# Summing two blocks by an accumulating transfer instead of on VectorE, in an FNet and SwiGLU kernel on one core

## The chip, the core and the metric

The kernel runs on one core of a Trainium2 chip. The metric is the device time of one execution in microseconds; three runs of the kernel before took 674.59 to 674.76, median 674.68. The engines are TensorE (PE; PEld is its loading of weights), VectorE (DVE), ScalarE (ACT), GpSimd (POOL) and SyncE (SP), which here only issues transfers. Transfers are issued by SP, POOL and ACT, each into a queue of its own, and carried out by 16 DMA engines that all queues share.

## The reference

```python
g = sigmoid((x * gate_w).sum(-1))                      # x: 2048 x 512, float32
a, b = x @ dft_hid_re.T, x @ dft_hid_im.T
y = dft_seq_re @ a - dft_seq_im @ b                    # two 2048 x 2048 transforms
h = silu(x @ w1) * (x @ w3)                            # 512 x 1376 each
return g * y + (1 - g) * (h @ w2)
```

Everything is float32. The two transforms commute; the kernel applies the one along the sequence first, with real and imaginary matrix, and the one along the hidden dimension to its results.

## The kernel before, in words

A float32 product is made of three float32r products: each operand is split into a high part (ScalarE, `high`, line 110) and a low part (VectorE, `low`, line 113), and `mm3` adds high by high, high by low and low by high. On top of that each product of 2 x 2 blocks is made with seven block products instead of eight, in Winograd's way, so that sums of blocks such as T1 = B12 + B11 are needed as operands.

The work has three phases: gate and up products of the feed-forward part (up to about 207 us), the sequence transform (block numbers 0 to 3 of the kernel's list of eight, kind "F"), and then the down product ("H", blocks 4 and 5) and the transform along the hidden dimension ("Y", 6 and 7). The change touches the "F" blocks 1 to 3.

An "F" block has 28 steps: seven products in the order P1, P5, P6, P3, P7, P2, P4 (block 0 has P2 ahead of P7), each over four pieces q = 0 to 3 of the contraction. A step has 12 matmuls of 128x512 and one moving operand "z", 128x1024 in high and low part (`ZT`, tiles `zo`, four buffers). The operands come from the four raw blocks B11, B12, B21, B22 of the transform's matrix (input `cc`), 512 KB per piece, in the tiles `RAW` (shown as B in the profile). Product P5, steps 4 to 7 of a block, uses T1 = B12 + B11, summed in B12's own tile; P6 uses T2 = T1 + B22 in the same tile; P7 uses T3 = T2 - B11, so B11 itself is kept; P4 uses T4.

The order of the work is written out by hand. Step m of all steps first runs the list of things that are due (`todo`), then issues its matmuls, and then `advance(m)`, which prepares later steps: `load_c(m + 8)` issues the loads that are due for step m + 8, on SP's queue, as far as tiles are free; `sum_c(m + 4)` makes the sum for step m + 4 on VectorE; `split_c(m + 3)` splits the operand of step m + 3. Since there are four z buffers, the high part for step m + 3 waits until the matmuls of step m - 1 are through.

The loads' list `LOADS` gives each raw piece a step by which it is due: the four of B12 of a block become due in the three steps before its P5 and the first of it, and are asked for up to eight steps earlier.

GpSimd's queue carries in these blocks the results: `spill` (line 818) stores the four results of a block into `zsp`, in the order zu, zp, zs, zc (in block 0 zs comes ahead of zp); zc is the last thing of a block's last step, after `advance`; `gates` (lines 769 and 770) stores the gates, once in block 0 and once in block 1; and in blocks 1 and 2 `late_store` (line 800) stores pre-split weights for the later phases, from the `todo` list and so ahead of the step's `advance`. Each of these transfers waits on GpSimd for the engine that made its data, and all that stands behind it in the program waits with it.

Of the kernel before, what the change touches and what calls it, by code (L numbers as in the profile page):

```python
# [10 lines left out]
ALU = mybir.AluOpType  # L11
# [4 lines left out]
F = 1376  # L16
# [17 lines left out]
def fnet_swiglu_gate_kernel(  # L34
# [21 lines left out]
    nc = tc.nc  # L56
# [41 lines left out]
    def wide(name):  # L98
        return take(F4, [P, 1024], F32, name)
# [4 lines left out]
    def free(*tiles):  # L104
        for t in tiles:
            _, places, at = HELD.pop(id(t))
            places.append(at)
# [490 lines left out]
    for k in range(LOOK + 2):  # L598
# [18 lines left out]
    KIND = "F" * NTB + "HHYY"  # L617
# [3 lines left out]
    STEPS = [(blk, q, k, form) for blk, nq in enumerate(NQ) for k, form in ORDER[blk]  # L621
             for q in range(nq)]
# [8 lines left out]
    LEAD = 3  # L631
# [4 lines left out]
    RAW, ZT = {}, {}  # L636
# [3 lines left out]
    def z_rows(tb, k):  # L640
        return zsp[(tb * 4 + k) * P : (tb * 4 + k + 1) * P, :]

    def block(blk, k, q):
        if KIND[blk] == "F":
            return cc[blk, ("B11", "B12", "B22", "B21").index(k), q]
        if KIND[blk] == "H":
            return hsp[blk - NTB, ("B11", "B12", "B21", "B22").index(k), q]
        return z_rows(2 * (blk - NTB - 2) + (k in ("B12", "B22")), 2 * (k in ("B21", "B22")) + q)

    def cols(blk, q, form):  # L650

        return 512 if KIND[blk] == "H" and q == NQ[blk] - 1 else 1024

    def done(m, j):
        blk, q, k, form = STEPS[m]
        b = DONE[j].get(form)
        if b:
            free(RAW.pop((blk, b, q)))

    def sum_c(m):  # L660


        if not 0 <= m < len(STEPS):
            return
        blk, q, k, form = STEPS[m]
        b = {"T1": "B11", "T2": "B22", "T4": "B21"}.get(form)
        if b:
            n = cols(blk, q, b)
            t = RAW[blk, PLACE[form], q][:, :n]
            nc.vector.tensor_add(t, t, RAW[blk, b, q][:, :n])  # L670
        elif form == "T3":
            n = cols(blk, q, form)
            t = RAW[blk, "B11", q][:, :n]
            nc.vector.tensor_sub(t, RAW[blk, "B12", q][:, :n], t)  # L674
        done(m, 0)

    def split_c(m, parts_of=(0, 1)):
        if not 0 <= m < len(STEPS):
            return
        blk, q, k, form = STEPS[m]  # L680
        src = RAW[blk, PLACE.get(form, form), q]
        if 0 in parts_of:
            ZT[m] = parts(f"zo{m}")
        t = ZT[m].rearrange("p h a n -> p h (a n)")
        n = cols(blk, q, form)
        if 0 in parts_of:
            high(t[:, 0, :n], src[:, :n])
        if 1 in parts_of:
            low(t[:, 0, :n], t[:, 1, :n], src[:, :n])
            done(m, 1)  # L690

    def load_c(m):
        while LOADS and LOADS[0][0] <= m and F4:
            _, blk, k, q = LOADS.pop(0)
            r = RAW[blk, k, q] = wide(f"{k}_{blk}_{q}")
            n = cols(blk, q, k)
            nc.sync.dma_start(r[:, :n], block(blk, k, q)[:, :n])

    def advance(m):
        load_c(m + LEAD + AHEAD)  # L700
        sum_c(m + LEAD + 1)
        split_c(m + LEAD)

# [47 lines left out]
    high_a(NG - 1)  # L751
    low_a(NG - 1)
    advance(-1)
    load_score(0)

# [118 lines left out]
    def step(m):  # L874
# [30 lines left out]
        for r in range(2):  # L905
            sl = slice(r * P, (r + 1) * P)
            for dst, some, new in banks_of(r) if steps else ():
                for n, zn in steps:
                    for i in range(ni):
# [4 lines left out]
                            some)  # L914
        free(zt)
        advance(m)
        if q < NQ[blk] - 1:
            return
# [155 lines left out]
    for i, (src, sp, p) in enumerate(late):  # L1074
        blk, b = 1 + i // 3, i % 3
# [106 lines left out]
```

## Time and profile before

| | us |
|---|---|
| median of three runs | 674.68 |
| profiled execution | 674.39 |
| its span, first to last instruction | 672.6 |
| PE busy in the span | 667.5 |
| DVE busy | 577.5 |
| ACT busy | 369.9 |
| POOL busy | 61.8 |

Busy times come from the profile's page, which describes one execution. A row of the groups or of the timeline names the engine, the line of the kernel, the operation and `out<-in` by the program's tile names; many operations are recorded at the line of a helper (110, 113, 124, 697), so tiles tell them apart. "POOLq" and "SPq" are issues of transfers, and the last number in such a row is the time in us from issue to landing. "<-" behind a row's idle time names what ended it. In the tables by stretch, each engine's busy time is followed by the number of its instructions, and the last three columns are the granted share of TensorE's clock, the mean busy share of the 16 DMA engines and the bytes that they moved in GB/s.

### The profile page before, as it was taken

What the parts mean: (1) busy time and instruction counts of PE and PEld (TensorE: products, weight loads), DVE (VectorE), ACT (ScalarE), POOL (GpSimd) and SP (SyncE); (2) the same over time, 40 slices, a digit from 0 to 9 for tenths busy, and PEclk for the clock granted to TensorE, in tenths of its full rate; (3) what the DMA queues carried; (4) which work ended last, traced back from release to release, by engine and by line L of the source; (5) the groups of instructions that cost most, each with busy time, mean ns of one, the idle gap of its engine ahead of it and who ended that gap; (6) DMA issues with size and microseconds to landing.
All of it is one profiled execution on the core that took longest, in us unless ns stands there. A gap on an engine that the chain in (4) does not pass through costs nothing.

```text
span 672.6 us, 8611 instructions
## 1 busy us (share of the span) xinstructions
PE 667.5 (99%) x3101; PEld 580.5 (86%) x3101; DVE 577.5 (86%) x684; ACT 369.9 (55%) x471; POOL 61.8 (9%) x114
## 2 busy tenths in 40 slices
PE   9999999999999999999999999999999999999997
PEld 6888888888888888888888888888888888888886
DVE  6979877787679999988999799869798698798896
ACT  6765556656546874465454655444446446445452
POOL 0011112121110000101120101000000010010000
PEclk9999999999999999999999999999999999999999
DMA  7675655599986957744697267619889795784942
GB/s 296 217 300 223 236 216 208 203 352 376 424 358 249 363 186 239 249 154 158 234 379 293 83 255 274 280 34 355 303 332 228 255 357 170 312 299 175 340 126 94
DMA packets 46010, 171.23 MB, mean 255 GB/s; under 512 B 5520, under 2 KB 5904, under 8 KB 42256
## 3 DMA queue, kind: packets, MB, share of 16 engines
q1 hardware_dynamic: 33376, 118.90, 49.8%
q0 software_dynamic: 12160, 51.13, 19.4%
q10 hardware_dynamic: 432, 0.66, 0.3%
q8 instruction: 24, 0.39, 0.2%
q14 instruction: 18, 0.15, 0.1%
HBM read 115.34 MB, written 55.32 MB: 254 GB/s over the span
## 4 chain that ended last, share of the span: by engine, by line
PE 99%; DMA 1%; ACT 0%; SPq 0%; issue 0%
PE P L124 68%; PE X L124 16%; PE Z L124 8%; PE Y L124 4%; PE C L124 2%; DMA xs_B<-xt 1%; PE V L124 0%; PE P4left L124 0%; ACT xo L110 0%; ACT zc L835 0%; SPq L223 0%
## 5 line engine op out<-in xcount | busy, mean ns | idle before, releaser
L124 PE MATMUL P<-zo,a 128*128 128x512 f32 x1344 | 290.3, 379 | 0.0
L110 ACT ACTIVATE zo<-B 128x1024 fp32r<-128x1024 f32 (+1 forms) x182 | 185.5, 1022 | 182.8 <-PE P L124 99.9
L124 PEld LDWEIGHTS P<-zo,a 128*128 128x128 f32 x1344 | 253.9, 189 | 36.2
L113 DVE TENSOR_TENSOR zo<-B,zo 128x1024 fp32r<-128x1024 f32 (+1 forms) x182 | 213.8, 1180 | 33.1 <-ACT zo L110 32.4
L670 DVE TENSOR_TENSOR B<-B,B 128x1024 f32<-128x1024 f32 (+1 forms) x78 | 91.8, 1177 | 0.1
L124 PE MATMUL P<-zo,H 128*128 128x512 f32 x420 | 91.3, 379 | 0.0
L124 PEld LDWEIGHTS P<-zo,H 128*128 128x128 f32 x420 | 79.2, 189 | 11.8 <-issue 0.7
L124 PE MATMUL X<-xo,wb 128*128 128x512 f32 x378 | 88.7, 379 | 0.0
L124 PEld LDWEIGHTS X<-xo,wb 128*128 128x128 f32 x378 | 71.3, 189 | 10.4 <-DMA wb<-wbsp 0.2
L124 PE MATMUL P<-zo,Y 128*128 128x512 f32 (+1 forms) x336 | 71.6, 375 | 0.0
L124 PEld LDWEIGHTS P<-zo,Y 128*128 128x128 f32 x336 | 62.7, 189 | 8.7
L385 ACT ACTIVATE h<-X 128x512 f32<-128x512 f32 x21 | 12.5, 596 | 36.0 <-PE X L124 36.0
L323 POOL DMA_DIRECT2D hsp<-h x40 | 21.9, 547 | 112.0 <-DVE h L374 66.6
L124 PE MATMUL Z<-xo,wb 128*128 128x512 f32 x126 | 30.9, 380 | 0.0
L674 DVE TENSOR_TENSOR B<-B,B 128x1024 f32<-128x1024 f32 (+1 forms) x26 | 30.6, 1178 | 0.0
L124 PE MATMUL Z<-xo,wa 128*128 128x512 f32 x126 | 30.6, 379 | 0.0
L124 PE MATMUL X<-xo,wa 128*128 128x512 f32 x126 | 30.5, 379 | 0.0
L124 PE MATMUL Y<-xo,wa 128*128 128x512 f32 x126 | 30.5, 379 | 0.0
L124 PEld LDWEIGHTS Z<-xo,wb 128*128 128x128 f32 x126 | 23.7, 189 | 3.7 <-DVE xo L113 0.4
L124 PEld LDWEIGHTS Y<-xo,wa 128*128 128x128 f32 x126 | 23.8, 189 | 3.4
L124 PEld LDWEIGHTS Z<-xo,wa 128*128 128x128 f32 x126 | 23.8, 189 | 3.4
L124 PEld LDWEIGHTS X<-xo,wa 128*128 128x128 f32 x126 | 23.8, 189 | 3.4
(158 smaller groups left out, 549.0 us busy)
## 6 DMA issues: line engine op xcount, KB each, us to landing
B<-cc SPq DMA_DIRECT2D x64, 512.0 KB, 6.3
hsp<-h POOLq DMA_DIRECT2D x40, 256.0 KB, 4.0
wbsp<-wb POOLq DMA_DIRECT2D x8, 1024.0 KB, 4.2
wb<-wbsp SPq DMA_DIRECT2D x8, 1024.0 KB, 8.1
B<-hsp SPq DMA_DIRECT2D x16, 512.0 KB, 8.5
B<-zsp SPq DMA_DIRECT2D x16, 512.0 KB, 7.4
ws<-w SPq DMA_DIRECT2D x11, 512.0 KB, 5.6
H<-w2sp SPq DMA_DIRECT2D x5, 1024.0 KB, 8.5
```

Source lines behind the costliest of these rows:

```text
L110: nc.scalar.activation(hi, src, AF.Copy)
L113: nc.vector.tensor_sub(lo, src, hi.bitcast(F32))
L124: nc.tensor.matmul(ps.rearrange("p (n a) -> p n a", a=2), u, turns(v)[:, some], **kw)
L323: nc.gpsimd.dma_start(hsp[g, b + k, j // 2, :, j % 2 * 512 : (j % 2 + 1) * 512], h)
L385: nc.scalar.activation(g1, x, AF.Silu)
L670: nc.vector.tensor_add(t, t, RAW[blk, b, q][:, :n])
L674: nc.vector.tensor_sub(t, RAW[blk, "B12", q][:, :n], t)
```

## The change

For the blocks 1 to 3 of kind "F", and the form T1 alone, `sum_c` does nothing. Instead a new function `add_c`, called in `advance` two steps ahead of where the sum stood and between the loads and the sums, issues a transfer on GpSimd's queue that reads B11 from HBM a second time and adds it into the tile of B12. That is 12 transfers of 512 KB in place of 12 instructions of VectorE. GpSimd has to wait for B12's load before it issues one, and ScalarE and VectorE wait for its landing before they split the sum. The T1 sums of block 0 and of the blocks of the other kinds stay on VectorE.

```diff
+    def by_dma(blk, form):
+        return KIND[blk] == "F" and blk > 0 and form == "T1"
+
+    def add_c(m):
+
+        if not 0 <= m < len(STEPS):
+            return
+        blk, q, k, form = STEPS[m]
+        if by_dma(blk, form):
+            nc.gpsimd.dma_start(RAW[blk, "B12", q], block(blk, "B11", q), accum_op=ALU.add)
+
     def sum_c(m):
...
         b = {"T1": "B11", "T2": "B22", "T4": "B21"}.get(form)
-        if b:
+        if by_dma(blk, form):
+            pass
+        elif b:
             n = cols(blk, q, b)
...
     def advance(m):
         load_c(m + LEAD + AHEAD)
+        add_c(m + LEAD + 3)
         sum_c(m + LEAD + 1)
         split_c(m + LEAD)
```

## The prediction

> **What bounds the kernel now.** I read the page first, then the chain of waits, then the busy time by stretches. On the page the chain that ended last lies on TensorE nearly everywhere:
>
> ```profile
> span 672.6 us, 8611 instructions
> PE 667.5 (99%) x3101; PEld 580.5 (86%) x3101; DVE 577.5 (86%) x684; ACT 369.9 (55%) x471; POOL 61.8 (9%) x114
> ...
> PE 99%; DMA 1%; ACT 0%; SPq 0%; issue 0%
> ```
>
> In order of time (start, length, what), that chain holds one unbroken run of matmuls from the start of the sequence transform on, and the matmuls of its four blocks fill their stretch:
>
> ```profile
> 206.95 325.92 PE P L124 x1510
> ```
>
> ```profile
> 206.95:497.03 290.08, 290.08 (x1345) 253.93 (x1345) 14.77 (x23) 18.49 (x32) 1.00 0.66 244
> ```
>
> The four blocks have 4 x 28 = 112 steps of 12 matmuls, so a step takes 290.08 / 112 = 2.590 us, and step m starts at 206.95 + 2.590 m. By block (columns: stretch, length, then PE, PEld, DVE, ACT and POOL busy, granted clock, DMA share, GB/s):
>
> ```profile
> 207.00:279.50 72.50, 72.50 (x337) 63.41 (x336) 70.95 (x75) 46.14 (x53) 3.74 (x7) 1.00 0.74 261
> 279.50:352.00 72.50, 72.50 (x337) 63.48 (x337) 66.90 (x76) 41.54 (x49) 9.46 (x18) 1.00 0.64 238
> 352.00:424.70 72.70, 72.70 (x338) 63.66 (x338) 66.89 (x72) 37.43 (x44) 6.71 (x13) 1.00 0.63 240
> 424.70:497.00 72.30, 72.30 (x337) 63.31 (x336) 59.40 (x57) 33.33 (x36) 2.14 (x4) 1.00 0.64 236
> ```
>
> TensorE has no gap in any block, so nothing that VectorE gives back there can shorten the run. The question is only whether the new transfers land before TensorE asks for their sums.
>
> **What is removed.** In blocks 1 to 3, 4 sums each: 12 of the 72 instructions of this row.
>
> ```profile
> L670 DVE TENSOR_TENSOR B<-B,B 128x1024 f32<-128x1024 f32 x72 | 87.7, 1218 | 0.1
> L113 DVE TENSOR_TENSOR zo<-B,zo 128x1024 fp32r<-128x1024 f32 x168 | 204.3, 1221 | 31.3 <-ACT zo L110 30.6
> ```
>
> 12 x 1.218 = 14.6 us of VectorE, 4.9 us a block. Beside a TensorE that never waits this is worth 0; it cannot be less than 0, nor more while PE reads 72.50 of 72.50.
>
> **What is added: 12 issues on GpSimd.** A plain issue there takes 0.53 to 0.55 us (start, length, what; idle time before it in brackets):
>
> ```profile
> 277.67 0.53 POOL L818 DMA_DIRECT2D zsp<-zp  x1 [3.07 <-DVE zp L816]
> 281.14 0.53 POOL L818 DMA_DIRECT2D zsp<-zc  x1 [2.94 <-DVE zc L816]
> ```
>
> ```profile
> 349.35 0.53 POOL L800 DMA_DIRECT2D dsp<-late_0l  x1 [0.93 <-DVE u2p L177]
> 350.63 0.55 POOL L800 DMA_DIRECT2D dsp<-late_1h  x1 [0.74 <-ACT late_1h L110]
> 351.69 0.55 POOL L800 DMA_DIRECT2D dsp<-late_1l  x1 [0.51 <-DVE late_1l L113]
> 355.17 0.54 POOL L818 DMA_DIRECT2D zsp<-zc  x1 [2.93 <-DVE zc L816]
> ```
>
> ```profile
> 418.27 0.54 POOL L818 DMA_DIRECT2D zsp<-zs  x1 [8.59 <-DVE zs L816]
> 425.88 0.55 POOL L818 DMA_DIRECT2D zsp<-zc  x1 [7.08 <-DVE zc L816]
> ```
>
> If an adding issue costs one to two plain ones, 12 take 6 to 13 us of an engine that is busy 9%; worth 0. The order matters more. `add_c` runs in the last two steps of the block before and the first two of its own, so the queue reads: zp, add 0, add 1, zc, add 2, add 3 (block 1); late_0l, add 0, late_1h, late_1l, add 1, zc, add 2, add 3 (block 2, where the late stores stand ahead of `step` in the same turns); zs, add 0, add 1, zc, add 2, add 3 (block 3). The first adds go out at about 278.2, 349.9 and 419.
>
> The added wait is for the block B12 that is to be added to. The four B12 loads of blocks 1, 2 and 3 are issued from 259 to 264, 338 to 345 and 410.5 to 416.5, and land in (median):
>
> ```profile
> B<-cc SPq DMA_DIRECT2D x4, 512.0 KB, 5.3
> ```
>
> ```profile
> B<-cc SPq DMA_DIRECT2D x4, 512.0 KB, 8.6
> ```
>
> ```profile
> B<-cc SPq DMA_DIRECT2D x4, 512.0 KB, 8.0
> ```
>
> In blocks 1 and 2 they are there when GpSimd reaches the add. In block 3 it waits until about 419.5 and 421; behind it stands only zc, which isn't asked for before 425.88. Worth 0.
>
> **When the sums are needed.** ScalarE makes the high part of a block 3 steps ahead, and VectorE the low part behind it (1.22 us, row L113 above):
>
> ```profile
> 282.16 1.06 ACT L110 ACTIVATE zo<-B 128x1024 fp32r<-128x1024 f32 x1 [1.58 <-PE P L124]
> ```
>
> That is step 32, the first with T1 of block 1 (its matmuls start at 206.95 + 82.88 = 289.83). The sum may come late by up to the cushion, and must land by the step's start less 1.06 + 1.22 = 2.3 us: 287.5, 290.1, 292.7, 295.3 in block 1 (steps 32 to 35), 360.0, 362.6, 365.2, 367.8 in block 2 (60 to 63), 432.6, 435.2, 437.8, 440.3 in block 3 (88 to 91). From issue to need there are only 9 to 13 us. A sum that is late holds up ScalarE and VectorE, whose next work (the copies of P1, the T2 sums) has 4 steps or more in hand, and TensorE, by what is missing.
>
> **When they land.** From the end of one block into the next the DMA engines are full, and then idle (columns as above):
>
> ```profile
> 289.00:294.00 5.00, 5.00 (x25) 4.36 (x25) 3.81 (x4) 4.29 (x7) 0.00 (x0) 1.00 0.00 0
> ...
> 349.00:358.00 9.00, 9.00 (x43) 7.87 (x43) 9.00 (x10) 4.83 (x5) 2.17 (x4) 1.00 1.02 404
> ...
> 419.00:425.20 6.20, 6.20 (x30) 5.44 (x29) 4.50 (x5) 2.76 (x3) 0.00 (x0) 1.00 1.03 413
> ...
> 432.00:440.00 8.00, 8.00 (x39) 7.01 (x38) 7.29 (x8) 4.24 (x5) 0.00 (x0) 1.00 0.01 3
> ```
>
> Full, they move about 0.41 MB a us, so 512 KB (0.524 MB) take 1.28 us. Call the work of one adding transfer c times that of a plain one of its size. No row shows one. It can't be below c = 1 (0.524 MB come in from HBM as in a load of B) and two whole transfers, c = 2, are my upper end. I take 1.5: a plain packet is read and written, this one is read twice and written, three passes for two.
>
> [...]
>
> What lies before each queue, in MB, in three stretches (282 to 289, 358 to 368, 425.2 to 435; q1 is SyncE's, q0 GpSimd's):
>
> ```profile
> q1 hardware_dynamic: 505, 1.55, 54.8%
> q0 software_dynamic: 288, 1.05, 36.6%
> ```
>
> ```profile
> q1 hardware_dynamic: 858, 2.86, 77.8%
> q0 software_dynamic: 33, 0.09, 2.7%
> ```
>
> ```profile
> q1 hardware_dynamic: 679, 2.19, 55.6%
> q0 software_dynamic: 144, 0.52, 13.1%
> ```
>
> I let the two queues share the engines half and half while both have work, serve GpSimd's in its order, and give 0.5 us from the last byte to the landing (block 1's 2.60 MB are out at 282 + 6.3 = 288.3; its zc, issued at 281.14, took 7.7):
>
> ```profile
> zsp<-zc POOLq DMA_DIRECT2D x1, 512.0 KB, 7.7
> ```
>
> *Block 1, from 282.* Ahead are zp (0.52) and 1.55 of q1. With c = 1.5 add 0 is through when q0 has moved 1.31 and q1 as much: 2.62 / 0.41 = 6.4, landing 288.9, late by 1.4. Add 1: (2.10 + 1.55) / 0.41, 291.4, late by 1.3. Add 2, behind zc: (3.41 + 1.55) / 0.41, 294.6, late by 1.9. Add 3: 296.5, 1.2. Lateness within a block isn't summed, since each shift of TensorE moves the later dates too: the block costs its maximum, **1.9**.
>
> *Block 2, from 358.* The engines are full before it, so add 0 (landing at about 358 to 360) only pushes 0.79 MB of others past 358. Ahead of add 1's end are then 0.09 + 0.52 x (2 x 1.5 - 1) = 1.14, with as much of q1: 5.6 us, 364.1, late by 1.5. Add 2: 2.45 twice, 12.0 us, 370.5, late by 5.3. Add 3: (3.23 + 2.86) / 0.41 = 14.9, 373.4, late by **5.6**.
>
> *Block 3, from 425.2*, when zs, issued at 418.27, is in:
>
> ```profile
> zsp<-zs POOLq DMA_DIRECT2D x1, 512.0 KB, 6.9
> ```
>
> Add 0: 2 x 0.79 / 0.41, 429.5; add 1: 433.4; both in time. Add 2, behind zc: (2.88 + 2.19) / 0.41, 438.1, late by **0.3**; add 3 in time.
>
> Sum: 1.9 + 5.6 + 0.3 = 7.8 us. With c = 1: 0.1 + 1.4 + 0 = 1.5. With c = 2: 3.8 + 8.2 + 2.2 = 14.2. The profiled execution took 674.39 (span 672.6 and 1.8 around it), 0.3 below the median of 674.68. Forecast 674.4 + 7.8 = **682.2 us**, slower.
>
> **The rivals.** *Hidden.* The adds land in time, and nothing waits: 674.4 to 675. For it: at c = 1 the sum misses by 1.5 us only, and a share above half for GpSimd's queue would take that away. Against it: from 282 to 289 that queue had 36.6% beside 54.8, and in block 2 TensorE's date falls amid full engines. This is the case that ends on the other side: not slower, decided where block 2's add 3 lands by 367.8, some 11.5 us after its issue. Chance 0.25.
>
> [...] Each block then stalls by the working above: 674.4 + 14.2 = 688.6. [...] Chance 0.25. Dearer still (c = 3, block maxima 8.9, 13.2 and 7.4 by the same working): 704, chance 0.08.
>
> *VectorE was the hidden limit* and 14.6 us off it shorten the run. Against it stand the four rows without a gap. By more than 0.2%: chance 0.03.
>
> *The change doesn't do what it says*, in that GpSimd's queue, not the engines, sets the landing: an issue of several us would make add 1 late in every block alike. For it nothing; chance 0.02, with the slower ones.
>
> **How the numbers follow.** The forecast, c from 1 to 1.8, has 0.37: 675.9 to 686. This kernel's runs can tell about 0.2%, 1.35 us, from no change. Same holds the hidden rival, 0.25; faster 0.03; slower the rest, 0.37 + 0.25 + 0.08 + 0.02 = 0.72. The range takes in the hidden case and c = 2 with 3 us for the halving of the shares: 674.3 to 692.
>
> **What would show it.** Each step right: gaps of TensorE just before steps 32 to 34, 61 to 63 and 90, none elsewhere in the blocks; ScalarE's L110 waiting there for a DMA and not for TensorE; adding transfers that take 9 to 17 us to land in blocks 1 and 2; L670 with 60 instructions of 128x1024 instead of 72; zc landing some 3 us later. Wrong: landings below 9 us with PE still at 72.50 a block (hidden), or GpSimd's issues well above 0.55 us. If block 2 doesn't lose more than block 1, the sharing that I assumed is wrong, whatever the sum.

## The result, and the profile after

The changed kernel takes 690.86 us (median, 690.48 to 691.20) beside 674.72 before: a ratio of 1.0238, 95% interval 1.0225 to 1.0251, 16.1 us slower. I had forecast 682.2 with a range of 674.3 to 692.0: the direction and the range hold, the size of the loss is a little over twice the forecast.

The page of the changed kernel: TensorE's busy time rises by 7 us and its span by 16, and the chain is no longer one of matmuls alone.

```profile
span 688.7 us, 8635 instructions
PE 674.6 (98%) x3101; PEld 582.8 (85%) x3101; DVE 563.7 (82%) x672; ACT 368.6 (54%) x471; POOL 72.5 (11%) x126
...
PE 64%; issue 17%; DMA 10%; DVE 4%; POOL 3%; ACT 1%; SPq 0%; POOLq 0%; ACTq 0%; DVEq 0%
```

VectorE has its 12 sums less (60 of 128x1024, 72 before), and its busy time falls from 577.5 to 563.7 us. That is the whole gain. The groups by shape of the changed kernel:

```profile
L683 DVE TENSOR_TENSOR B<-B,B 128x1024 f32<-128x1024 f32 x60 | 73.0, 1217 | 0.1
```

Busy time by stretches of the changed kernel (columns as in the prediction): the gaps of TensorE, and a granted clock below 1, which the profile of the kernel before doesn't show in these blocks.

```profile
279.50:352.00 72.50, 70.64 (x318) 60.71 (x317) 58.15 (x66) 37.20 (x45) 10.70 (x18) 0.98 0.73 240
352.00:424.70 72.70, 68.54 (x301) 57.91 (x300) 55.95 (x63) 34.88 (x42) 11.68 (x19) 0.95 0.66 224
```

Who waits: ScalarE for the adding transfers, 11 of 12 times, as the list of waits has it.

```profile
ACT zo L110 <- DMA B<-cc: 45.5, 11, 9.2
```

In order of time, ScalarE's splitting of block 1's first three T1 operands; before the change the first of these rows began at 282.16 and waited for TensorE.

```profile
290.34 1.06 ACT L110 ACTIVATE zo<-B 128x1024 fp32r<-128x1024 f32 x1 [9.24 <-DMA B<-cc]
293.58 1.06 ACT L110 ACTIVATE zo<-B 128x1024 fp32r<-128x1024 f32 x1 [2.18 <-DMA B<-cc]
...
297.39 1.06 ACT L110 ACTIVATE zo<-B 128x1024 fp32r<-128x1024 f32 x1 [1.81 <-DMA B<-cc]
```

TensorE's timeline around the three places (start, length, what, idle time before):

```profile
207.32 2.97 PE L124 MATMUL P<-zo,a 128*128 128x512 f32 x13
...
291.45 0.48 PE L124 MATMUL P<-zo,a 128*128 128x512 f32 x1 [1.08 <-ACT zo L110]
292.71 9.48 PE L124 MATMUL P<-zo,a 128*128 128x512 f32 x34 [0.78 <-DVE zo L113]
...
372.40 0.80 PE L124 MATMUL P<-zo,a 128*128 128x512 f32 x1 [2.66 <-ACT zo L110]
...
383.12 4.15 PE L124 MATMUL P<-zo,a 128*128 128x512 f32 x18 [0.46 <-DVE zo L113]
...
453.78 0.48 PE L124 MATMUL P<-zo,a 128*128 128x512 f32 x1 [0.67 <-ACT zo L110]
...
458.73 3.50 PE L124 MATMUL P<-zo,a 128*128 128x512 f32 x15 [0.78 <-DVE zo L113]
```

The loss of each block comes out of these rows and the prediction's dates. Step 61 was due at 206.95 + 61 x 2.590 = 364.94, and TensorE stands idle for it from 372.40 - 2.66 = 369.74: 4.8 us lost by then, of which 0.5 came before the first add (the transform's first matmul is at 207.32 here and was at 206.79; other profiled runs below have it up to 207.6). Step 90 was due at 440.05 and TensorE is idle from 453.11: 13.1 lost. The second matmul of step 91 was due at 442.86 and starts at 458.73: 15.9, and from there on the chain is one run again. So block 1 cost 4.3, block 2 8.3 and block 3 2.8 us, each to about 0.3 (the first two dates are read at the end of a matmul, the last at the start of one).

### The profile page after: what moved, and what is told of

Same layout as the page of the kernel before. It is cut to its first block, busy times and chain, and to the rows that moved or that the text cites. A ratio compares the mean times of both kernels' runs of the same rounds, so it can differ in the third digit from the quotient of the medians.

```text
span 688.7 us, 8635 instructions
## 1 busy us (share of the span) xinstructions
PE 674.6 (98%) x3101; PEld 582.8 (85%) x3101; DVE 563.7 (82%) x672; ACT 368.6 (54%) x471; POOL 72.5 (11%) x126
## 4 chain that ended last, share of the span: by engine, by line
PE 64%; issue 17%; DMA 10%; DVE 4%; POOL 3%; ACT 1%; SPq 0%; POOLq 0%; ACTq 0%; DVEq 0%
PE P L124 34%; PE X L124 16%; PE Z L124 8%; DMA B<-cc 7%; PE Y L124 4%; DVE zo L113 2%; DMA xs<-xn 2%; PE C L124 2%; DMA s1g<-gs 1%; POOL B L669 1%; DVE B L687 1%; POOL dsp L814 1%; DMA xs_B<-xt 1%; ACT zo L110 1%; POOL zsp L832 1%
## 5 line engine op out<-in xcount | busy, mean ns | idle before, releaser
L124 PE MATMUL P<-zo,a 128*128 128x512 f32 x1344 | 297.6, 384 | 8.2 <-ACT zo L110 4.4
L124 PEld LDWEIGHTS P<-zo,H 128*128 128x128 f32 x420 | 79.2, 189 | 11.8 <-issue 0.7
L124 PEld LDWEIGHTS X<-xo,wb 128*128 128x128 f32 x378 | 71.3, 189 | 10.4 <-DVE u L368 0.2
L683 DVE TENSOR_TENSOR B<-B,B 128x1024 f32<-128x1024 f32 (+1 forms) x66 | 77.1, 1168 | 0.1
L385 ACT ACTIVATE h<-X 128x512 f32<-128x512 f32 x21 | 12.5, 596 | 34.5 <-PE X L124 34.5
L687 DVE TENSOR_TENSOR B<-B,B 128x1024 f32<-128x1024 f32 (+1 forms) x26 | 30.6, 1176 | 0.0
```

Of the source, the lines that this page charges most:

```text
L124: nc.tensor.matmul(ps.rearrange("p (n a) -> p n a", a=2), u, turns(v)[:, some], **kw)
L385: nc.scalar.activation(g1, x, AF.Silu)
```

## The experiments

My theory after the result: an adding transfer takes twice the DMA engines' time of a plain one, lands late where the engines are full (their mean busy share was 1.04 from 282 to 289 and 1.06 from 289 to 294 in the changed kernel), and costs its lateness and nothing else. Rivals: the wait chain through GpSimd costs, whatever is moved; GpSimd's queue takes too few transfers at a time; adding transfers slow something else wherever they are.

### A plain copy in the same place

```diff
-            nc.gpsimd.dma_start(RAW[blk, "B12", q], block(blk, "B11", q), accum_op=ALU.add)
+            nc.gpsimd.dma_start(RAW[blk, "B12", q], block(blk, "B11", q))
```

> The 12 transfers stay where they are, but copy B11 over B12 instead of adding to it (so T1 is B11, and the operands of P5, P6 and P7 in three blocks are other numbers; all else is computed). Theory (an adding transfer takes twice the DMA engines' time of a plain one, 2.6 us instead of 1.3, and lands late because the engines are full there): with one plain pass the working of the prediction gives stalls of 0.1 + 1.4 + 0 us, 676 us, and q0's time in the queue table grows by 12 x 1.28 us of all engines. Rival (the extra hop through GpSimd's queue with its wait for B12, whatever the transfer moves): within 3 us of the changed kernel, 688 or more.

This kernel leaves the addition out. Measured: 679.13 us, ratio 1.0069 (1.0052 to 1.0085). The 12 transfers cost 4.4 us as plain copies and 16.1 as adding ones. What one transfer takes of the engines comes from the queue tables (packets, MB, share of the 16 engines' span): q0, GpSimd's queue, before, in the changed kernel, and here. The last two have the same packets and bytes.

```profile
q0 software_dynamic: 12160, 51.13, 19.4%
```

```profile
q0 software_dynamic: 13888, 57.43, 23.5%
```

```profile
q0 software_dynamic: 13888, 57.43, 21.5%
```

Adding: (0.235 x 688.7 - 0.194 x 672.6) / 12 = 2.61 us of all 16 engines. Plain: (0.215 x 677.5 - 0.194 x 672.6) / 12 = 1.27, the 1.28 of the prediction. So c = 2.06. (The shares are rounded, which leaves about 0.06 us open in each of the two; the other runs with 12 adds give 2.57 to 2.70 by the same sum.) On GpSimd an adding issue takes 0.87 us and a plain one 0.545 (in ns, min/median/max of 12, the changed kernel's row first):

```profile
L669 POOL DMA_DIRECT2D B<-cc x12: 835/872/1075, 279.1 to 442.7; - x12
```

```profile
L669 POOL DMA_DIRECT2D B<-cc x12: 540/545/560, 279.4 to 432.1; - x12
```

The rival falls: the same hop and the same wait for B12 cost 4.4, not 16. But 4.4 is more than the 1.5 of my working at c = 1; the experiment's 676 was a miss.

### More descriptor space for GpSimd

```diff
-    nc = bacc.Bacc("TRN2", ..., dynamic_dma_scratch_size=1024)
+    nc = bacc.Bacc("TRN2", ..., dynamic_dma_scratch_size=1792)
```

> The changed kernel with 1792 instead of 1024 bytes of descriptor space for GpSimd's transfers. In the changed kernel's trace GpSimd issues an add about 0.3 us after an older transfer of its queue has landed (286.68 after 286.38, 290.55 after 290.24, 360.09 after 359.78, 364.40 after 364.10, 367.65 after 367.35, 442.71 after 442.40), as if no more could be in flight. Theory (full engines set the landings): the issues come earlier, the landings and the time stay, 689 to 691 us. Rival (the limit on what is in flight sets the landings): the third and fourth add of a block, held up by 2 to 8 us, come in time, and 5 us or more are won, 686 or less.

Measured: 692.09 us, ratio 1.0262 (1.0247 to 1.0277), no faster than the changed kernel's 690.86. The hold on the issues is real (4.4 us before add 2 and 3.0 before add 3 in the first rows below, none with more space) and costs nothing here. GpSimd's timeline in block 1, in the changed kernel and then with more space (the row of line 669 with x2 holds two adds):

```profile
278.20 0.53 POOL L832 DMA_DIRECT2D zsp<-zp  x1 [3.06 <-DVE zp L830]
279.06 1.81 POOL L669 DMA_DIRECT2D B<-cc  x2 [0.34 <-issue]
281.67 0.57 POOL L832 DMA_DIRECT2D zsp<-zc  x1 [0.80 <-DVE zc L830]
286.68 0.85 POOL L669 DMA_DIRECT2D B<-cc  x1 [4.44 <-issue]
290.55 0.83 POOL L669 DMA_DIRECT2D B<-cc  x1 [3.01 <-issue]
```

```profile
281.59 0.56 POOL L832 DMA_DIRECT2D zsp<-zc  x1 [0.94 <-DVE zc L830]
282.30 1.74 POOL L669 DMA_DIRECT2D B<-cc  x2
```

Adds 2 and 3 are issued at 282.3 and 282.9 instead of 286.7 and 290.6, and take about that much longer to land. From issue to landing, over the block's four (min, median, max), the changed kernel first:

```profile
DMA to landing us min/median/max: 9.3/10.9/13.7
```

```profile
DMA to landing us min/median/max: 11.7/14.7/17.2
```

### Three steps earlier

```diff
-        add_c(m + LEAD + 3)
+        add_c(m + LEAD + 6)
```

> The adds are issued three steps (7.8 us) earlier in the program, ahead of the results' stores of the block before. Theory (late landing alone costs): block 1's adds find idle engines and are in time; in blocks 2 and 3 the B12 loads (landing from 347 and from 419 on) bound the gain, with stalls of 0 to 1 us each; 675 to 677.5 us. Rival (the adding transfers slow the other engines or the loads wherever they are): at most half of the 16 us come back, 683 or more.

Measured: 677.58 us, ratio 1.0042 (1.0027 to 1.0057). 13.3 of the 16.1 us come back with the same 12 adds. Some 0.85 of the rest is a later start of the transform (207.64 for 206.79); the remainder stands mostly in block 3, where TensorE's timeline has its only larger waits:

```profile
441.84 0.48 PE L124 MATMUL P<-zo,a 128*128 128x512 f32 x1 [0.52 <-ACT zo L110]
443.10 2.86 PE L124 MATMUL P<-zo,a 128*128 128x512 f32 x12 [0.78 <-DVE zo L113]
```

### T4 instead of T1

```diff
-        return KIND[blk] == "F" and blk > 0 and form == "T1"
+        return KIND[blk] == "F" and blk > 0 and form == "T4"
...
-            nc.gpsimd.dma_start(RAW[blk, "B12", q], block(blk, "B11", q), accum_op=ALU.add)
+            nc.gpsimd.dma_start(RAW[blk, "B12", q], block(blk, "B21", q), accum_op=ALU.add)
```

> T4 (B21 added into B12's tile, steps 24 to 27 of a block) is made by the adding transfer in blocks 1 to 3, and T1 by VectorE as before. Same number and size of adds, issued where the DMA engines are nearly idle. Theory: each add lands some 4 to 5 us after its issue (a plain store of this size lands in 2.9 there, and 1.3 more for the second pass), long before ScalarE needs it; 674.5 to 675.2 us, as before the change. Rival (an add is slow by itself, whatever else runs): landings near the 11.6 us of the changed kernel, and 680 or more.

Measured: 694.00 us, ratio 1.0288 (1.0273 to 1.0303): by the number, and by landings of 11.8 us in the median, a win for the rival. GpSimd's timeline in block 1 points to another reason:

```profile
325.65 0.93 POOL L669 DMA_DIRECT2D B<-cc  x1 [0.27 <-issue]
...
330.23 0.87 POOL L669 DMA_DIRECT2D B<-cc  x1
335.51 0.55 POOL L832 DMA_DIRECT2D zsp<-zp  x1 [4.41 <-DVE zp L830]
...
339.19 0.89 POOL L669 DMA_DIRECT2D B<-cc  x1 [1.99 <-PE P L124]
342.39 0.87 POOL L669 DMA_DIRECT2D B<-cc  x1 [2.30 <-issue]
```

The stretch isn't idle: late stores and the next block's loads are in it. And the third add stands behind the store of zp, which waits for VectorE until 335.5, and behind two late stores, and then 2.0 us more. The profile names TensorE for these, but the issue comes 0.3 us after an older late store has landed (issued at 329.57, 9.3 us), so it may be the limit on what is in flight; more space was not tried in this place. Step 54, which needs it, was due at 206.95 + 139.9 = 346.8, so by 344.5 at ScalarE. Issued at 339.19 it took 12.4 us to land, 7.1 late. I had looked at the steps of the adds and not at the queue ahead of them, though the prediction had done that for T1. The next run tests this reason.

### T4, three steps earlier

```diff
-        add_c(m + LEAD + 3)
+        add_c(m + LEAD + 6)
```

(on the kernel of the run before)

> T4 by the adding transfer, as in the run before, but issued three steps earlier, ahead of the stores that it stood behind. In that run's trace the adds of blocks 1 and 2 were not in an idle stretch, as I had thought: the third was issued at 339.19 and 420.53, behind two stores and 5 and 12 us after the step that it belongs to, and landed 7 us or more after its need. Theory (an add costs nothing where it lands before its need, and its whole lateness where it doesn't): issued before about 327, 400 and 471, all land 3 us or more before their need; 674.5 to 675.6 us. Rival (adding transfers cost time by themselves, in T4's place or by slowing the loads of the next block): 677 or more.

Measured: 674.63 us, ratio 0.9995 (0.9987 to 1.0004): no change from the kernel before. TensorE is without a gap in all three blocks again:

```profile
279.50:352.00 72.50, 72.50 (x338) 63.48 (x337) 62.53 (x72) 41.16 (x49) 12.72 (x21) 1.00 0.71 244
352.00:424.70 72.70, 72.70 (x339) 63.66 (x338) 62.89 (x68) 37.57 (x43) 10.60 (x17) 1.00 0.80 273
424.70:497.00 72.30, 72.30 (x337) 63.31 (x336) 55.53 (x53) 33.49 (x36) 5.75 (x8) 1.00 0.75 264
```

Yet the adds are as slow as ever. Issue to landing of the 12 adds (min, median, max), in the run before (+19.3 us) and in this one (0):

```profile
DMA to landing us min/median/max: 5.5/11.8/13.9
```

```profile
DMA to landing us min/median/max: 6.2/11.1/17.4
```

That pair settles it: 12 adds with the same work and much the same times from issue to landing cost 19 us or nothing, by when they were issued against when their sums are asked for. Nor does the time that they free on VectorE bring anything.

### A wait of TensorE without any adding transfer

On the kernel before:

```diff
-            high(t[:, 0, :n], src[:, :n])
+            for _ in range(1 + {(1, 0, "T1"): 7, (2, 0, "T1"): 11}.get((blk, q, form), 0)):
+                high(t[:, 0, :n], src[:, :n])
```

> The kernel before, without any adding transfer; ScalarE makes the high part of the first T1 operand 8 times over in block 1 and 12 times over in block 2 (same data, same place), so that TensorE must wait there about 1 and 4 us. The changed kernel's trace has the granted clock at 0.5 for 3.41 us in block 1 and 6.83 us in block 2, after such waits. Theory (the wait itself brings the half clock): the clock falls to 0.5 for 3.4 us or more after block 2's wait, and the time is 681 to 683 us, 1.7 us or more above the two waits' sum. Rival (the adding transfers' traffic brings it): the clock stays at 1.0, and the time is 679 to 680.5.

Measured: 686.77 us, ratio 1.0177 (1.0163 to 1.0191). The waits came out longer than meant (some 2 and 7 us; 9 splits in a row took 9.62 us of ScalarE, and I had reckoned with less), and the time is above both of the ranges expected, so it tells nothing by itself. The clock does: in block 2 it is at one half for 6.8 us, with the DMA engines idle (share 0.00).

```profile
369.80:376.60 6.80, 4.42 (x10) 3.19 (x11) 4.91 (x5) 5.04 (x7) 0.00 (x0) 0.50 0.00 0
```

So here a wait of TensorE, 6.73 us, brought it without any adding traffic. TensorE's timeline there: 15 matmuls in 5.30 us after a wait of 6.73. In the run three steps earlier 12 took 2.86, so 15 take about 3.5 at full clock, and the half clock cost 1.8.

```profile
371.71 0.80 PE L124 MATMUL P<-zo,a 128*128 128x512 f32 x1 [6.73 <-ACT zo L110]
372.97 5.30 PE L124 MATMUL P<-zo,a 128*128 128x512 f32 x15 [0.46 <-DVE zo L113]
```

In the changed kernel it lies in these two stretches:

```profile
293.70:297.10 3.40, 3.40 (x10) 2.70 (x9) 1.23 (x1) 1.88 (x2) 0.00 (x0) 0.51 1.08 224
372.20:379.00 6.80, 6.13 (x13) 4.10 (x13) 1.69 (x2) 1.71 (x4) 0.00 (x0) 0.50 1.06 281
```

Each is followed by a further wait for an add of the same block (ScalarE's at 297.39, TensorE's at 383.12, above). A slow step that ends before the next operand is there costs nothing; so there the half clock is inside the lateness, not on top of it. In block 2 the chain of waits has the last add, from issue to landing:

```profile
367.65 13.02 DMA B<-cc
```

It landed at 380.67; with 2.3 us for the two splits that is 383.0, and TensorE goes on at 383.12. That is read from the trace, not tried.

### No late store ahead of block 2's adds

On the changed kernel:

```diff
-        blk, b = 1 + i // 3, i % 3
-        n = (10, 17, 24)[b]
+        blk, b = 1 + i // 2, i % 2
+        n = (10, 17)[b]
```

> The changed kernel with the late weights prepared two to a block in blocks 1, 2 and one in block 3, instead of three and two, so that no late store stands at the end of block 1 ahead of block 2's adds. Theory (what lies ahead on GpSimd's queue and on the engines sets an add's landing): block 2, which lost 8.2 us in the changed kernel's trace, loses about 3 as block 3 does, blocks 1 and 3 stay at 4.3 and 3.1; 684 to 687 us. Rival (the adds and the wait for B12 are enough, the stores don't matter): 689 or more.

Measured: 687.52 us, ratio 1.0189 (1.0175 to 1.0203), 3.3 below the changed kernel and half a microsecond above the range expected. TensorE's timeline, blocks 2 and 3:

```profile
373.89 0.48 PE L124 MATMUL P<-zo,a 128*128 128x512 f32 x1 [1.74 <-ACT zo L110]
375.15 7.12 PE L124 MATMUL P<-zo,a 128*128 128x512 f32 x25 [0.78 <-DVE zo L113]
...
450.95 0.48 PE L124 MATMUL P<-zo,a 128*128 128x512 f32 x1 [1.78 <-ACT zo L110]
452.21 10.15 PE L124 MATMUL P<-zo,a 128*128 128x512 f32 x38 [0.78 <-DVE zo L113]
```

Idle from 450.95 - 1.78 = 449.17 for step 90, due at 440.05, it had lost 9.1 by the end of block 2. With the 4.3 of block 1 and a start of the transform like the changed kernel's, block 2 cost about 4.5 instead of 8.3. So nearly half of it goes with the late weights at the end of block 1; the edit moves their loads and splits along with their stores, and these weren't tried apart. Block 3 cost more than in the changed kernel (4.7 for 2.8: the profiled span of 686.4 is 13.8 longer than that of the kernel before). In both blocks a half clock of 3.4 us came with the waits, which I hadn't counted on:

```profile
374.70:378.10 3.40, 2.95 (x7) 2.41 (x8) 2.62 (x3) 2.11 (x3) 0.00 (x0) 0.50 0.24 94
453.20:456.60 3.40, 3.40 (x10) 2.68 (x9) 2.50 (x4) 1.91 (x2) 0.00 (x0) 0.50 0.00 0
```

Here it seems to have cost time. The last add of block 2, issued at 362.77, took 13.1 us to land; 2.3 later, at 378.2, the second matmul of step 63 could start, 7.8 us after its date of 370.34, yet 9.1 were lost. In block 3 the same sum, 439.02 + 14.0 + 2.3 = 455.3, is 12.5 after the date of step 91's second matmul (442.86), and 13.8 were lost. So I estimate the half clock's price at about one us in each of the two blocks, on top of the adds' lateness.

### Three steps earlier, blocks 1 and 2 alone

```diff
-        return KIND[blk] == "F" and blk > 0 and form == "T1"
+        return KIND[blk] == "F" and 0 < blk < 3 and form == "T1"
...
-        add_c(m + LEAD + 3)
+        add_c(m + LEAD + 6)
```

> Adds issued three steps earlier, and only in blocks 1 and 2 (8 transfers; block 3's T1 sums on VectorE). With all three blocks that timing left 2.3 us of waits in block 3 and 0.4 in block 2. Theory (only lateness costs): 674.6 to 675.6 us, no change from before that can be told; the 9.7 us of VectorE that it frees bring nothing, since TensorE has no gap to fill. Rival (an early add delays the loads around it, at a price elsewhere): 676.5 or more. A gain over the kernel before, 673.5 or less, would show that VectorE did limit it.

Measured: 675.24 us, ratio 1.0006 (0.9997 to 1.0015), no change that can be told. The 2.3 us more that the early adds of all three blocks cost go with those of block 3, though in the profiled executions 0.9 of them is the earlier start of the transform here (206.73 for 207.64). No run beats the kernel before: its TensorE has no gap left to win in these blocks.

## Why the prediction was right or wrong, point by point

**What bounds the kernel, and the worth of the removed sums: right.** TensorE's unbroken run made 14.6 us of VectorE worth nothing. The two runs that hide the adds (674.63 with all 12 of T4, 675.24 with 8 of T1) show it: neither is faster than the kernel before.

**The place of the loss: right.** Waits come at the T1 steps of blocks 1, 2 and 3, most in block 2, none elsewhere in the blocks; ScalarE's row 110 waits for the transfers; they take 9.3 to 13.7 us (I had said 9 to 17); the dates by which a sum must land held.

**The price of one add: wrong, and this is the step that failed.** I took c = 1.5. The three passes for two behind it were my estimate, and no run shows them; the runs show 2.06: 2.61 us of all engines against 1.27 for a copy. With c = 2, to which I gave 0.25, the working has blocks of 3.8, 8.2 and 2.2 and 688.6 us; measured are 4.3, 8.3 and 2.8, and 690.86. So with the right c the forecast's own working comes within 2.3 us. With c = 2 the working has the four adds of block 1 land at 290.1, 292.7, 296.5 and 299.1; with the transform's 0.5 us later start that is 290.6 to 299.6, and the trace has the first and last at 290.2 and 299.8. Why an add takes twice a copy, no run here shows. I had no row against c = 2 and chose the middle between the ends.

**The sharing of the engines: a smaller miss.** At c = 1 the working gives 1.5 us and the copy cost 4.4 (0.8 of that is its later start of the transform). With that run's later dates its four copies of block 1 land 0.5 to 1.3 us after the working's times (289.7 to 295.2 for 288.4 to 294.7), which counts little at 8 us and all at 1.5. Which of the three assumptions is too kind (half and half, 0.41 MB a us from the first moment, 0.5 us to land), no run separates. So the "hidden" rival could not have come true at this place, even at a copy's price.

**The price at GpSimd: right, the order behind it less so.** Twelve issues of 0.87 us are 10.4 us (I had 6 to 13), on an engine with room for them. An issue of 0.87 is well above 0.55, which the prediction had named as a sign of being wrong; it came and cost nothing that the runs show. The prediction did not have that issues are held back until older transfers land (in the changed kernel add 2 of block 1 for 4.4 us, until 0.3 us after zp's landing). And zc lands 6 us later than before (294.9 for 288.8), not 3, again for c. The rival that GpSimd's queue sets the landing is refuted by the run with more space, in this place.

**The half clock wasn't foreseen.** Its 10.2 us make some 5 of the 7.3 us by which the busy time of these matmuls grew (297.6 for 290.3 in their group) but, as far as the trace can tell, none of the loss; in the run without the late stores it cost, by my estimate, about one us in each of blocks 2 and 3.

## What to carry to other kernels

Moving work from an engine that has slack to the DMA engines was free in these runs only where the transfers landed before their need: look at what stands ahead of the issue on its queue, count what the engines have ahead of it in bytes, and price an adding transfer at two copies (2.61 against 1.27 us of all engines for 512 KB). Whether a transfer was fast mattered less than when it was issued: for T4, landings 6 to 17 us after the issue cost nothing three steps earlier, and landings 6 to 14 us after it cost 19 us where they were late. And where the bounding engine has no gap, such a move has no gain to set against its risk: with 14.6 us off VectorE and TensorE without a wait in these blocks (all 12 adds of T4 early), the ratio was 0.9995.

## What the runs showed of the hardware

An adding transfer of 512 KB that found the engines nearly free landed in 5.5 us, where a store of the same size landed in 3.0 (the issues at 325.65 and 324.84 of the T4 run; no packet moved from 324.0 to 325.0 and from 325.5 to 325.8). GpSimd's issues were held back until an older transfer of its queue had landed: with 1024 bytes of descriptor space the third add of block 1 waited 4.4 us and went out at 286.7, 0.3 us after zp (issued at 278.20, 8.2 us) had landed, and with 1792 bytes it went out at 282.3 without a wait. TensorE's granted clock stood at one half for 3.4 us (block 1 of the changed kernel, blocks 1, 2 and 3 of the run without the late stores) or 6.8 us (block 2 of the changed kernel and of the run with the longer splits), with waits that sum to between 1.8 and 7.2 us. Waits that sum to 1.9 us (1.08 and 0.78, block 1 of the changed kernel) or 1.8 us (1.02 and 0.78, block 1 of the run without the late stores) were enough, while 2.2 us (0.67 and twice 0.78, block 3 of the changed kernel) and 1.8 us (1.05 and 0.77, block 1 of the run with the longer splits) brought none. What decides between these stays open.
